# Sliding-window attention with sinks, followed by a GELU MLP: token pairs in the q/k loads, a new order of first loads, the first GEMM2 by row-block pairs, and DMA transposes

## The chip, the cores and the metric

The kernel runs on one core of one Trainium2 chip. The metric is the device time of one execution in microseconds. The kernel before took 263.49 us (median of 4 runs in the rounds shared with the changed kernel). Engine names are as in the profile: PE (TensorE matmuls), PEld (its weight loads), DVE (VectorE), ACT (ScalarE), POOL (GpSimd), SP (SyncE, whose queue issues nearly all DMAs; "SPq"). A **span** is the time from the first to the last instruction of a profiled run.

## The reference

Batch 4, 8 heads, 768 tokens, head size 64, in float32. Each query sees the last 128 keys and the first 4 ("sinks"). The result goes through an MLP with exact GELU.

```python
scores = scale * q @ k.T
keep   = is_sink | ((rel >= 0) & (rel < 128))
a      = softmax(where(keep, scores, -1e9))
x      = (a @ v)  -> (3072, 512)      # tokens x (head, dim)
out    = gelu(x @ w_in) @ w_out       # 512 -> 2048 -> 512
```

## The kernel before

Tokens are handled in 12 **groups** g of 256 tokens. Two groups make a **chunk** c of 512 tokens, so there are six chunks, 0 to 5. For each chunk, GEMM1 (64 matmuls, GELU on ACT) is followed by GEMM2 (64 matmuls), and the attention of the next chunk is interleaved in slots after every four matmuls of GEMM2. While GEMM1 of chunk c runs, q, k and v of chunk c+1 are cast to bf16, and q and k are transposed on PE:

```python
def qk_transpose(g, pp, eng=nc.vector):          # twice per group: 2 x 8 PE transposes
    ...
    nc.tensor.transpose(pt[:, a, w, e, :], src[:, e, 2*p:2*p+2, :]..., ident)
    ...
    copy(eng, qkt, pt)                           # PSUM -> SBUF, on DVE

def x_transpose(g, p):                           # per group and pair of heads: 2 PE transposes
    for e in range(2):
        nc.tensor.transpose(tp[:, e*P:(e+1)*P], x4[:, 2*e:2*e+2, :]..., ident)
    nc.vector.tensor_copy(out=XT[c][:, p, o:o+Q2], in_=tp)
```

Loads go through ten staging tiles of 512 KB, in the order of one list `stream`. `pump()` issues as many as have a free staging tile. A tile becomes free when its cast has been written into the program:

```python
def pump(limit=len(stream)):
    while head[0] < min(limit, len(stream)):
        n = head[0]
        if n >= NST and not freed[n - NST]: return
        ...                                      # q, k, v: two DMAs each, runs of 256 bytes
```

Instructions stay in program order on each engine, DMA issues on SP too.

The softmax here doesn't subtract the row's maximum and nothing guards it: scores larger than these inputs give would overflow.

## Time and profile before

| | kernel before |
|---|---|
| span of the profiled run | 261.3 us |
| GEMM1 of chunk 1 starts | 74.89 us |
| four periods (start of GEMM1 of chunks 1 to 5) | 39.4, 38.5, 37.8, 39.4 us |
| from GEMM1 of chunk 5 to the end | 31.2 us |
| PE busy | 88% |

The starts are read from the chain of waits, the profile's list of the work that led to the last instruction. A wait counts only if the engine that waits is on that chain at that time. Before 75 us that is mostly DMA, after it PE. The prediction below shows the lines.

### The profile page before, as it was taken

Reading aid. Unit: us, or ns where it says so; the run is one execution under the profiler, and the core shown is the slowest. Engines: PE = TensorE matmul, PEld = TensorE weight load, DVE = VectorE, ACT = ScalarE, POOL = GpSimd, SP = SyncE. Lnnn points to the kernel's source line nnn. Section 1 sums busy time; section 2 is a strip of 40 time slices with the busy share of each in tenths; the row PEclk is TensorE's granted clock in tenths of the full one; section 3 lists DMA queues with packets and bytes.
Section 4 is the critical chain, followed back from the end, with each engine's and each line's share of the span. In section 5 each row is a group of like instructions: output and inputs, shape, how many; then the busy total and the mean of one; then the engine's idle time right before and its main releaser. Section 6 shows DMA issues by size and latency. Waiting matters only on the chain.

```text
span 261.3 us, 4320 instructions
## 1 busy us (share of the span) xinstructions
PE 230.7 (88%) x1734; PEld 118.2 (45%) x1764; DVE 122.1 (47%) x277; ACT 115.4 (44%) x120; POOL 32.4 (12%) x82
## 2 busy tenths in 40 slices
PE   0467699869999989999999999999999989999994
PEld 0235445325445535444535444545445445544441
DVE  0284844247844256844346734357643267610111
ACT  0556336555315585314575325585135666136300
POOL 7177500690000000002000000200000000000000
PEclk9998589999999999999999999999999999999999
DMA  8999999999999991129920146001210010110022
GB/s 155 218 273 348 257 229 271 387 240 229 200 221 283 228 168 43 43 96 225 203 48 34 43 129 112 3 2 41 80 40 3 0 40 4 75 48 0 0 83 80
DMA packets 84756, 33.84 MB, mean 129 GB/s; under 512 B 75520, under 2 KB 79616, under 8 KB 84736
## 3 DMA queue, kind: packets, MB, share of 16 engines
q1 hardware_dynamic: 82656, 33.04, 54.8%
q10 hardware_dynamic: 2080, 0.52, 1.1%
q8 instruction: 14, 0.23, 0.4%
q14 instruction: 6, 0.05, 0.1%
HBM read 27.26 MB, written 6.29 MB: 128 GB/s over the span
## 4 chain that ended last, share of the span: by engine, by line
PE 58%; DMA 13%; DVE 8%; SPq 7%; ACT 7%; issue 5%; POOL 1%; another core or an unknown queue 0%; ACTq 0%; POOLq 0%; DVEq 0%
PE big L399 26%; PE po L418 21%; SPq L170 7%; ACT et L304 5%; DMA st<-in_moe_w_out_dram 5%; DMA st<-in_moe_w_in_dram 4%; DMA st<-in_v_dram 4%; PE qkps L244 3%; DVE osb L427 3%; PE big L295 2%; PE bank L383 2%; DVE x L368 1%; DVE et L315 1%; PE bank L356 1%; ACT gt L407 1%
## 5 line engine op out<-in xcount | busy, mean ns | idle before, releaser
L418 PE MATMUL po<-WOUT,gt 128*128 128x512 bf16 x365 | 91.5, 380 | 5.3 <-POOL WOUT L193 3.3
L399 PE MATMUL big<-xt,WIN 128*128 128x512 bf16 x373 | 88.0, 383 | 0.7 <-issue 0.2
L407 ACT ACTIVATE gt<-big 128x1024 bf16<-128x1024 f32 x48 | 49.1, 1023 | 88.4 <-PE big L399 87.2
L399 PEld LDWEIGHTS <-WIN 128*128 128x128 bf16 x384 | 37.0, 99 | 41.6 <-issue 2.4
L304 ACT ACTIVATE et<-big 128x1024 bf16<-128x1024 f32 (+1 forms) x48 | 44.5, 954 | 19.8 <-PE big L295 11.5
L418 PEld LDWEIGHTS <-gt 128*128 128x128 bf16 x384 | 33.1, 98 | 41.2 <-issue 10.9
L308 DVE TENSOR_TENSOR et<-et,mask 128x1024 bf16<-128x1024 bf16 x32 | 24.2, 758 | 28.7 <-ACT et L304 28.6
L427 DVE COPY osb<-po 128x512 f32<-128x512 f32 x24 | 16.5, 688 | 39.7 <-PE po L418 39.6
L193 DVE COPY qkt<-qkps 128x1024 bf16<-128x1024 bf16 x22 | 15.2, 691 | 35.3 <-PE qkps L244 35.3
L256 POOL COPY sk<-qkt 64x4 bf16<-64x4 bf16 x32 | 6.9, 215 | 129.0 <-DVE qkt L193 127.9
L244 PE MATMUL qkps<-ident,q 128*128 128x128 bf16 x96 | 13.2, 234 | 8.1 <-DVE q L193 7.9
L295 PE MATMUL big<-qkt 64*128 64x128 bf16 (+1 forms) x256 | 18.6, 249 | 2.0 <-ACT et L304 2.0
L368 DVE TENSOR_TENSOR x<-bank,rz 128x256 bf16<-128x256 f32 x44 | 18.7, 424 | 1.5
L356 PE MATMUL bank<-vo,et 128*128 128x65 bf16 x176 | 18.7, 198 | 0.2 <-POOL sk L256 0.2
L383 PE MATMUL bank<-ident,x 128*128 128x128 bf16 x88 | 12.9, 230 | 6.0 <-DVE x L368 5.9
L348 PE MATMUL bank<-vo,et 128*128 128x65 bf16 x148 | 17.2, 197 | 0.1
L383 PEld LDWEIGHTS <-x 128*128 128x128 bf16 x96 | 6.6, 101 | 22.5 <-DVE x L368 20.6
L356 PEld LDWEIGHTS <-et 128*128 128x128 bf16 x192 | 15.8, 103 | 2.0 <-issue 0.9
L348 PEld LDWEIGHTS <-et 128*128 128x128 bf16 x160 | 15.0, 103 | 0.9 <-DVE et L308 0.3
L244 PE MATMUL qkps<-ident,k 128*128 128x128 bf16 x96 | 13.2, 233 | 1.9 <-ACT k L191 1.9
L244 PEld LDWEIGHTS <-q 128*128 128x128 bf16 x96 | 8.9, 105 | 13.0 <-DVE q L193 7.9
L389 DVE COPY xt<-bank 128x256 bf16<-128x256 bf16 x44 | 12.5, 285 | 3.8 <-PE bank L383 3.8
(52 smaller groups left out, 146.5 us busy)
## 6 DMA issues: line engine op xcount, KB each, us to landing
st<-in_q_dram SPq DMA_DIRECT2D x24, 256.0 KB, 5.1
st<-in_v_dram SPq DMA_DIRECT2D x24, 256.0 KB, 4.9
out_dram<-osb SPq DMA_DIRECT2D x24, 256.0 KB, 2.0
st<-in_k_dram SPq DMA_DIRECT2D x22, 256.0 KB, 4.8
st<-in_moe_w_in_dram SPq DMA_DIRECT2D x8, 512.0 KB, 7.9
st<-in_moe_w_out_dram SPq DMA_DIRECT2D x8, 512.0 KB, 9.3
st<-in_k_dram ACTq DMA_DIRECT2D x2, 256.0 KB, 5.6
```

Source lines behind the costliest of these rows:

```text
L244: nc.tensor.transpose(pt[:, a, w, e, :], src[:, e, 2 * p : 2 * p + 2, :].rearrange("s h d -> s (h d)"), ident,)
L295: nc.tensor.matmul(ps[:, hl, c : c + n * P], lhsT=kb[r : r + D, :], rhs=qt(g, p)[r : r + D, e : e + n, :].rearrange("p e n -> p (e n)"), s ...
L304: nc.scalar.activation(out=et[:, :, c0:], in_=ps[:, :, c0:], func=AF.Exp, scale=att_scale)
L308: nc.vector.tensor_tensor(out=et.rearrange("p h (e n) -> p (h e) n", e=2), in0=et.rearrange("p h (e n) -> p (h e) n", e=2), in1=mask.unsqu ...
L348: nc.tensor.matmul(pov[:, e, hl, :], lhsT=et[:, hl, 2 * e * P : (2 * e + 1) * P], rhs=low[:, h, :], start=(i == 0), stop=False, skip_group ...
L356: nc.tensor.matmul(pov[:, e, hl, :], lhsT=et[:, hl, (2 * e + 1) * P : (2 * e + 2) * P], rhs=VO[g][:, e, h, :], start=(low is None), stop=True,
L368: nc.vector.tensor_tensor(out=x4, in0=pv4[:, :, 0:D], in1=rz.unsqueeze(2).to_broadcast((P, 4, D)), op=ALU.mult,)
L383: nc.tensor.transpose(tp[:, e * P : (e + 1) * P], x4[:, 2 * e : 2 * e + 2, :].rearrange("p h d -> p (h d)"), ident,)
L399: nc.tensor.matmul(ph[:, a, :], lhsT=WIN[:, t, ts(f, P)], rhs=XT[c][:, t, :], start=(t == 0), stop=(t == NKT - 1),)
L407: nc.scalar.activation(out=gt, in_=ph, func=AF.Gelu)
L418: nc.tensor.matmul(po, lhsT=GT[c, f // 2][:, f % 2, ts(m, P)], rhs=WOUT[:, f, :], start=(f == 0), stop=(f == NFT - 1),)
L427: nc.vector.tensor_copy(out=osb, in_=po)
```

## The change

The intent is to take transposes and copies off PE and DVE, to make loads cheaper, and to start sooner. The core of the diff, with cuts marked by "...":

```diff
-    for g in range(4):
-        stream += [("q", g), ("k", g), ("v", g)]
-    stream[6:6] = [("wi", j) for j in range(8)]
+    stream = [("q", 0), ("k", 0), ("q", 1), ("k", 1), ("v", 0), ("v", 1)]
+    stream += [("wi", j) for j in range(8)]
+    stream += [(kind, g) for g in (2, 3) for kind in "qkv"]
     stream += [("wo", j) for j in range(8)]
...
+                if kind == "v":                  # four DMAs of 64 partitions, every other row
+                    for e in range(2):
+                        for r in range(2):
+                            eng.dma_start(out=dst[HP*r : HP*(r+1), e, :, :],
+                                in_=src[:, e*P:(e+1)*P, :].rearrange("h (s r) d -> r s h d", r=2)[r])
+                else:                            # q, k: one DMA, two tokens per partition, 512 bytes
+                    eng.dma_start(out=st.rearrange("p (h c) -> p h c", h=H),
+                        in_=src.rearrange("h (p r) d -> p h (r d)", r=2))
...
+    def qk_dma(g):                               # groups 4 to 11: four per group
+        ...
+                nc.sync.dma_start(out=qkt[:, w, e]..., in_=cast["qk"[w], g][e*HP:(e+1)*HP]..., transpose=True)
...
+        elif p == NPAIR - 1:                     # in av(): x of groups 2 to 11, one per group
+            nc.sync.dma_start(out=xt_tile(g // 2)[:, o:o+2]..., in_=XG[g]..., transpose=True)
...
-            nc.sync.dma_start(out=out[r0 : r0 + P, :], in_=osb)
+            for r in range(2):                   # rows are even/odd tokens: two stores of 64 partitions
+                nc.sync.dma_start(out=out[r0 : r0 + P, :].rearrange("(s r) c -> r s c", r=2)[r],
+                    in_=osb[HP * r : HP * (r + 1), :])
...
+            if c == 0:   # after GEMM1 of chunk 0 has been emitted
+            mms = [(2 * a + m, f) for a in range(2) for f in range(NFT) for m in range(2)]
+        else:
+            mms = [(m, f) for m in range(4) for f in range(NFT)]
```

Constants are filled by DVE instead of POOL, and the exponential's table is loaded at the start. A function for warm-up matmuls is defined but never called.

## The prediction

> **What bounds the kernel now.** I read the page first: the busy row, then the 40 slices.
>
> ```profile
> PE   0467699869999989999999999999999989999994
> PEclk9998589999999999999999999999999999999999
> DMA  8999999999999991129920146001210010110022
> ```
>
> One slice is 261.3 / 40 = 6.5 us. After the first eight or so slices TensorE (PE) is nearly always busy; before that it is broken up. DMA is full for the first 15 slices (about 95 us), then mostly idle. So there are two regimes, and the 88% of PE on the page is an average over both. I cut the span at the starts of GEMM1 of each chunk, which the chain of waits gives (74.89, 114.33, 152.85, 190.67, 230.11 us), and asked for the busy time by stretch (columns: span, then PE, PEld, DVE, ACT, POOL busy, clock, DMA share, GB/s):
>
> ```profile
> 57.00:74.90 17.90, 16.62 (x152) 8.70 (x155) 11.72 (x33) 6.15 (x7) 1.30 (x5) 1.00 1.09 212
> 74.90:90.60 15.70, 15.60 (x96) 8.10 (x97) 7.07 (x11) 7.18 (x8) 0.00 (x0) 1.00 1.13 249
> 90.60:114.30 23.70, 22.11 (x213) 11.45 (x216) 13.37 (x35) 12.15 (x13) 0.00 (x0) 1.00 0.43 89
> 230.10:243.90 13.80, 13.75 (x65) 6.24 (x64) 0.69 (x1) 7.16 (x7) 0.00 (x0) 1.00 0.05 19
> ```
>
> A chunk's GEMM1 stretch (second row) is 15.7 us; the last chunk's (fourth row), which has no q/k transposes beside it, is 13.8 us, 64 matmuls at 0.216. The GEMM2-plus-attention stretch (third row) is 23.7 us, of which PE is idle 1.6. From 74.9 us on, PE sets the time: four chunk periods of 39.4, 38.5, 37.8 and 39.4 (mean 38.8), and a last stretch of 31.2.
>
> The idle 1.6 us has an owner. The waits of PE's weight loads, whole kernel:
>
> ```profile
> PEld L383 <- DVE x L368: 20.6, 37, 1.4
> ```
>
> L383 is the transpose of the attention output x. It waits on VectorE (DVE), which must mask, normalise and evict for the same slot.
>
> For the start I read the DMA queue's own order of issues (start, length, what):
>
> ```profile
> 40.38 5.00 SPq L180 DMA_DIRECT2D st<-in_moe_w_out_dram  x8
> 45.95 7.01 SPq L170 DMA_DIRECT2D st<-in_q_dram  x2
> ...
> 74.50 2.40 SPq L170 DMA_DIRECT2D st<-in_q_dram  x2
> 77.00 3.16 SPq L429 DMA_DIRECT2D out_dram<-osb  x4
> ```
>
> The first output tile was evicted by 59.5 us, yet its store is issued at 77.0: SyncE issues in program order, and ten loads (q4 to q7) stand in front. Today nobody waits for that store. I keep this in mind, because the change puts something urgent in its place.
>
> Rates, from the DMA view of 0 to 60 us in 40 slices of 1.5 us:
>
> ```profile
> GB/s 0 106 274 218 217 218 218 218 218 218 224 313 350 349 349 347 350 354 344 255 154 200 263 224 221 220 216 216 237 355 382 391 386 384 391 375 273 131 168 207
> ```
>
> The 218 plateaus are the q/k/v loads (256-byte runs), 350 is w_in (1 KB), 386 is w_out (2 KB). Per run and engine (16 x bytes / rate) this is 18.8, 46.8 and 84.9 ns, which is a straight line: 9.5 ns + 0.0367 ns per byte.
>
> **What the Trainium skill says.** (1) "DMA: Bandwidth & Descriptors", Specifications, gives 512 B as the minimum transfer for line rate. The trace agrees that 256 B is poor (218 against 386), but its line shows no step: it gives 28.3 ns, or 289 GB/s, at 512 B (estimate). (2) The same page, Queues, rings and completion order, says each DMA engine consumes its ring in order; the store at 77.0 us fits. (3) "Advanced Engine Details and Errata", X-Bar Transpose (TRN2), says transpose DMAs are as fast as regular ones, 350 to 400 GB/s, while the DMA page's table Latency and other measured facts has 261 GB/s for a non-contiguous case. This kernel has no such DMA, so no run here shows it; it is my weakest number. (4) "TensorE: Matmul & The Clock Gate", Part 1, says that after an idle window of about 3.4 us PE runs at half clock until about 3.4 us of work has passed. The trace agrees in kind: the granted clock is 0.59 between 30.5 and 36 us, after a stretch with gaps.
>
> **The change part by part.**
>
> *q/k transposes by DMA from chunk 2.* Groups 4 to 11 lose 8 x 16 = 128 PE transposes. The page's mean of 234 ns is latency; in the chain eight take 0.45 us, so a chunk saves 32 x 0.056 = 1.8 us of PE. This agrees with 15.7 - 13.8 = 1.9. All of it is on the path. Four chunks: 7.2 us. DVE also loses four 0.69 us copies per chunk, off the path.
>
> *x transposes by DMA from chunk 1.* 16 per chunk, a pair every 0.12 us in the timeline: 0.96 us of PE, on the path. With them goes the wait for DVE in front of them, about 1.5 us per chunk (PE idle of 1.6, 1.5, 1.1, 1.7 in the four GEMM2 stretches), and eight 0.285 us DVE copies. I count 2.4 us per chunk.
>
> So the period becomes 38.8 - 1.8 - 2.4 = 34.6 us; four periods save 17.
>
> *What comes back at each chunk start.* GEMM1 needs the whole x^T. The last AV is now in slot 11 of 16, followed by 20 matmuls x 0.216 = 4.3 us. Beside that run DVE's reciprocal and multiply (0.17 + 0.42, with hand-overs about 0.9), then SyncE's issue, and 256 KB through the transposer: 0.7 to 1.0 us by (3), plus about 2.0 us to landing, the page's median for a 256 KB store. That is 3.6 to 3.9 plus issue, against 4.3. I take 1 us lost per boundary, four boundaries: +4. The eight q/k transposes (128 KB each) have the 13.8 us of GEMM1 to hide in.
>
> *Token pairs and the new order.* A q or k tile of 512 KB costs 1.81 us in place of 2.41 (estimate from the line), 0.6 saved. v keeps 256-byte runs. SyncE must issue everything up to q7 before the first x transpose of chunk 1: the eight w_out casts pull in those loads before GEMM2(0) is emitted. Work in front: 15 q/k tiles x 1.81 + 7 v x 2.41 + 8 x 1.50 + 8 x 1.36 = 67.0 us, starting at 2. The same sum for the old kernel is 75.9 + 2 = 77.9, and its q7 finished issuing at 76.9, so the model holds. The new q7 is therefore in at about 69 to 70.5 us, and then come the transpose of group 2, two output tiles, and the transpose of group 3: x^T for chunk 1 at about 74, where GEMM1(1) starts at 74.9 today. By its own work PE would be ready at 62 to 66 (faster start of attention, no wait for w_out). It idles some 8 us, finds a halved clock and loses about 1.5. The better first loads thus buy almost nothing: 74 + 1.5 against 74.9.
>
> *GEMM2(0..4) by row-block pairs.* It lets the w_out blocks of chunk 0 be used as they land (waits of 3.3 us before w_out matmuls on the page), but that gain lies in the stretch which the queue now bounds. In later chunks it halves the pace at which GELU outputs are needed. Two evictions now fall together, covered by a slot of attention. I count 0.
>
> *Early Exp table load, memsets moved.* The 1.28 us table load at 7.9 us leaves the start; also absorbed. The warm-up function is defined and never called: 0.
>
> Sum: 74 + 1.5 + 4 x 34.6 + 4 + 31.2 = 249.1 us of span. The measured time is 263.88 - 261.3 = 2.6 above the span, so **251.7**.
>
> **Rivals.**
>
> A. The start is PE-bound after all: the x transposes are not held up behind loads, and GEMM1(1) begins at 62 to 66. For it: PE work alone ends there, and one fast queue would do it. Against: the store at 77.0. It would make about 240 to 243.
>
> B. DMA transposes are slow. At 3 us per 128 KB the eight q/k transposes take 24 us per chunk, SyncE's six loads (12 us) queue behind them, and the x transposes behind those: periods of 38 to 40 us, DMA taking PE's place as bound. For it: I have no measured duration. Against: both figures in (3). It makes 258 to 268.
>
> C. Transposes land in time but the masks and exponentials bind the GEMM2 stretch: exp 1.02 and DVE 0.69 + 0.17 + 0.42 = 1.28 us per slot, against 0.86 + 0.33 + 0.38 = 1.57 of PE. The margin is there, so at most 1 us per chunk: about 256.
>
> **Range and chances.** The period is certain to about 1 us (4 in all), the boundary wait 0 to 3 us each, the first x^T 70 to 78. Together 241 to 261. Below 258.6 is faster by 2%: only B, or C with a late start, prevents it. Faster 0.80, within 2% 0.16, slower 0.04.
>
> **What would show it.** GEMM1(1) starts at 72 to 76 us after several idle us of PE, released by a transpose DMA, with q7's load issued just before that; then periods of 34 to 36.5 us with GEMM1 stretches near 14 and hardly any PE wait on DVE's x; at each later chunk start a wait of about 1 us for the x transpose. The rate of q/k loads is near 289 GB/s. I am wrong if GEMM1(1) starts before 68 (A), if boundary waits exceed 3 us or attention waits for q/k transposes (B), or if exp or mask waits recur in the GEMM2 stretch (C).

## The result, and the profile after

The changed kernel took **255.38 us** (median of 4 runs, 254.93 to 256.1) against 263.49. The ratio is 0.9689, with a 95% interval of 0.9648 to 0.9729. It is the mean time of the one kernel's fast runs over that of the other's in the same rounds, so not quite the ratio of the medians. Executions over 1.5% slower than the fastest of the same kernel are left out of the means. The prediction was 251.7 with a range of 241 to 261. The direction and the range held, and the centre was 3.7 us too fast. (The profiled run was the slowest of the four: 256.1 us, span 254.1. The other spans were 252.9 to 253.5.)

The 40 slices of the changed kernel (6.35 us each):

```profile
PE   0686997878804999999999999999999999999992
PEclk9996899999965799999999999999999999999998
DMA  6999999999999579945669995593465213510133
```

Note the hole in PE in slices 12 and 13, the fallen clock in it and just after it, and the solid nines from there on. Here is the queue of SP around the hole (start, length, what):

```profile
70.08 0.98 SPq L195 DMA_DIRECT2D st<-in_q_dram  x1
71.16 2.72 SPq L428 DMA_TRANSPOSE xt<-xg  x1
73.98 2.47 SPq L484 DMA_DIRECT2D out_dram<-osb  x4
76.54 1.31 SPq L428 DMA_TRANSPOSE xt<-xg  x1
77.95 2.46 SPq L484 DMA_DIRECT2D out_dram<-osb  x4
```

L428 is the x transpose. Its first input was ready at 59.5 us, its second at 65.6 (the ends of the last multiply of groups 2 and 3 on DVE). They are issued at 71.16, right behind the load of q of group 7, and at 76.54, behind four stores. PE's waits say what this costs (who waited for whom, us in total, times, longest):

```profile
PE big L455 <- DMA xt<-xg: 10.5, 1, 10.5
```

There is one such wait in the whole kernel, 10.5 us long. The stretches from there on (span, then PE, PEld, DVE, ACT, POOL busy, clock, DMA share, GB/s):

```profile
79.68:96.35 16.67, 16.67 (x65) 6.95 (x65) 0.00 (x0) 7.16 (x7) 0.00 (x0) 0.83 0.72 143
...
117.98:132.20 14.22, 14.22 (x67) 6.26 (x65) 4.99 (x8) 7.16 (x7) 0.38 (x2) 1.00 0.59 97
132.20:152.34 20.14, 19.86 (x174) 9.89 (x172) 11.02 (x27) 11.04 (x12) 0.00 (x0) 1.00 1.19 220
```

The first row is GEMM1 of chunk 1: 16.67 us at a mean granted clock of 0.83, where 64 matmuls at full clock take 13.8. The other two are GEMM1 and GEMM2 of chunk 2: 14.2 and 20.1 us, with 0.28 us of idle PE in the latter. The chain of waits gives the starts of GEMM1 of chunks 2 to 5:

```profile
117.98 6.91 PE big L455 x32
...
152.34 6.91 PE big L455 x32
...
186.23 13.83 PE big L455 x64
...
221.51 13.81 PE big L455 x64
```

| | before | predicted | after |
|---|---|---|---|
| GEMM1 of chunk 1 starts | 74.89 | 74 | 79.68 |
| lost to the clock in it | 0 | 1.5 | 2.87 (16.67 - 13.8) |
| four periods, without that loss | 155.2 | 138.4 | 138.96 (35.43, 34.36, 33.89, 35.28) |
| waits at later chunk starts | - | 4 | 0 |
| last stretch | 31.2 | 31.2 | 32.6 |
| span | 261.3 | 249.1 | 254.1 |

The periods gave 16 us. The start took back 4.8, the clock 2.9 and the end 1.4.

### The profile page after: what moved, and what is told of

Read it like the earlier page. It is cut to its first block, busy times and chain, and to the rows that moved or that the text cites. A ratio compares the mean times of both kernels' runs of the same rounds, so it can differ in the third digit from the quotient of the medians.

```text
span 254.1 us, 3961 instructions
## 1 busy us (share of the span) xinstructions
PE 220.4 (87%) x1556; PEld 109.0 (43%) x1556; DVE 103.2 (41%) x237; ACT 114.8 (45%) x120; POOL 28.9 (11%) x47
## 4 chain that ended last, share of the span: by engine, by line
PE 61%; SPq 17%; DMA 11%; DVE 5%; issue 2%; ACT 2%; POOL 1%; DVEq 0%; ACTq 0%
PE po L472 30%; PE big L455 22%; SPq L188 7%; DMA st<-in_moe_w_in_dram 6%; SPq L296 4%; PE big L340 4%; SPq L195 3%; DMA st<-in_v_dram 2%; DMA st<-in_moe_w_out_dram 2%; SPq L484 2%; PE bank L404 2%; DVE osb L481 2%; ACT et L349 2%; PE bank L396 1%; PE bank L384 1%
## 5 line engine op out<-in xcount | busy, mean ns | idle before, releaser
L455 PE MATMUL big<-xt,WIN 128*128 128x512 bf16 x384 | 87.2, 388 | 10.5 <-DMA xt<-xg 10.5
L472 PE MATMUL po<-WOUT,gt 128*128 128x512 bf16 x384 | 93.4, 380 | 3.3 <-POOL WOUT L218 2.4
L472 PEld LDWEIGHTS <-gt 128*128 128x128 bf16 x384 | 33.3, 97 | 42.2 <-issue 10.2
L481 DVE COPY osb<-po 128x512 f32<-128x512 f32 x24 | 16.3, 688 | 40.3 <-PE po L472 34.7
L418 DVE TENSOR_TENSOR xg<-bank,rz 128x256 bf16<-128x256 f32 x44 | 18.7, 424 | 1.5
L360 DVE TENSOR_TENSOR et<-et,mask 128x768 bf16<-128x768 bf16 x16 | 9.0, 566 | 15.2 <-ACT et L349 14.6
L263 POOL COPY sk<-qkt 64x16 bf16<-64x16 bf16 x8 | 2.1, 269 | 111.1 <-DMA qkt<-k 110.8
L384 PE MATMUL bank<-vsk,ets 128*128 128x130 bf16 x60 | 12.3, 225 | 2.4 <-DVE vsk L251 1.3
L340 PEld LDWEIGHTS <-qkt 64*128 64x128 bf16 x256 | 7.7, 96 | 10.8 <-issue 7.5
L218 POOL CAST WOUT<-st 128x1024 bf16<-128x1024 f32 x8 | 9.4, 1186 | 15.0 <-DMA st<-in_moe_w_out_dram 14.8
L218 POOL CAST WIN<-st 128x1024 bf16<-128x1024 f32 x8 | 9.4, 1172 | 3.8 <-DMA st<-in_moe_w_in_dram 3.8
L415 DVE RECIPROCAL rz<-bank 128x4 f32<-128x4 f32 x44 | 7.8, 177 | 4.5 <-PE bank L404 3.9
L218 DVE CAST q<-st 128x1024 bf16<-128x1024 f32 x11 | 7.5, 686 | 4.9 <-DMA st<-in_q_dram 4.9
```

Of the source, the lines that this page charges most:

```text
L218: eng.tensor_copy(out=out, in_=in_)
L340: nc.tensor.matmul(ps[:, hl, c : c + n * P], lhsT=kt(gk, p, ek, rows), rhs=qt(g, p, e, n, rows), start=True, stop=True,)
L418: nc.vector.tensor_tensor(out=XG[g][:, :, 2 * p : 2 * p + 2, :], in0=pov[:, :, :, 0:D], in1=rz.rearrange("p (e h) -> p e h", e=2).unsqueez ...
L455: nc.tensor.matmul(ph[:, a, :], lhsT=WIN[:, t, ts(f, P)], rhs=XT[c][:, :, t, :], start=(t == 0), stop=(t == NKT - 1),)
L472: nc.tensor.matmul(po, lhsT=GT[c, f // 2][:, f % 2, ts(m, P)], rhs=WOUT[:, f, :], start=(f == 0), stop=(f == NFT - 1),)
L481: nc.vector.tensor_copy(out=osb, in_=po)
```

## The experiments

Each is an edit of the changed kernel, and each ratio is to the kernel before. "Start" below is the start of GEMM1 of chunk 1, 79.68 us in the changed kernel.

**e1_cap: fewer loads in front of the x transposes.** Is it the order in SP's queue?

```diff
                 take("wo", j, G_)
-                pump()
+                pump(32)          # also in the two side slots of chunk 0
...                                # after GEMM2 of chunk 0:
+        if c == 0:
+            pump(34)
...                                # in later chunks, side slot 1: pump() -> pump(34 + 6 * c)
```

> Edit: in chunk 0 the loads are capped so that only q4, k4, v4, q5 stand in front of the x transposes of chunk 1 on SyncE; k5 and v5 follow after the stores of chunk 0, later groups six per chunk. Theory Q (in-order queue): GEMM1 of chunk 1 starts at 69 to 71 us in place of 79.7, finds a warm clock and takes 13.9 us in place of 16.7; the span falls by 10 to 13 us to 241 to 244, ratio to the kernel before 0.92 to 0.93. Rival T (the transposes themselves are slow when the first ones run): the start stays at 77 us or later and the gain is under 3 us. Rival D (DMA bandwidth is the bound, the loads are only moved): the wait comes back as a wait for k5/v5 or for the q/k transposes in chunk 1, and the gain is under 5 us.

Measured: 246.56 us (three runs within 0.3 us, a fourth at 249.71), ratio 0.9378 (0.9317 to 0.9439), correct, span 244.5. SP's queue and the chain:

```profile
56.92 1.18 SPq L195 DMA_DIRECT2D st<-in_q_dram  x1
59.82 1.35 SPq L428 DMA_TRANSPOSE xt<-xg  x1
61.46 2.46 SPq L484 DMA_DIRECT2D out_dram<-osb  x4
65.87 1.23 SPq L428 DMA_TRANSPOSE xt<-xg  x1
```
```profile
69.48 13.83 PE big L455 x64
...
107.53 7.08 PE big L455 x32
```

The transposes are issued as soon as x is there, the start is 10.2 us earlier, and GEMM1 takes 13.83 us. The bytes loaded are the same. So the wait was one of order, as theory Q says. No run separates the order in which SP issues from the order in the DMA queue behind it. The gain stays just under the forecast 10 us (9.6 of span), because PE waits 2.8 us for x at the start of chunk 2: six loads, which now run later (SP issues them from 87 to 100 us), stand in front of that one.

**e2_x_pe: the x transposes of chunk 1 on PE.** The urgent work leaves the queue altogether.

```diff
-        if g < 2:
+        if g < 4:                 # and x_transpose(g, p) one slot after av(g, p)
             PO[g, p] = po
```

> Edit: the x transposes of chunk 1 alone (groups 2 and 3) are done by PE again; the order of loads is that of the changed kernel. Theory Q: nothing on PE's path hangs on SyncE's queue at the start, so GEMM1 of chunk 1 starts at 70 to 72 us; it pays 1 to 2.5 us for 16 PE transposes and their waits for DVE; the q/k transposes of group 4 are still issued only at about 80 us and may hold GEMM2 of chunk 1 by up to 3 us. Net gain 6 to 11 us, span 243 to 248. Rival T: about the same, since no transpose stands at the start. Rival D: under 5 us, because the loads still take the queue until 71 us and something else waits for them.

Measured: ratio 0.9404 (0.9352 to 0.9456), correct. The two fast runs took 248.8 and 247.2 us. The profiled run was slow (251.0), so its span is not compared. In it GEMM1 of chunk 1 starts at 70.55 us, as theory Q says (first line, from the chain), and this wait of PE appears for chunk 2 (second line):

```profile
70.55 13.83 PE big L456 x64
...
PE big L456 <- DMA xt<-xg: 5.1, 1, 5.1
```

With the loads untouched, the backlog meets the next x transposes instead. That would explain why it gains less than e1_cap, but I have the wait only from that slower run.

**e3_fill: dummy matmuls in the hole.** Is the slow GEMM1 of chunk 1 the clock?

```diff
+        if c == 0:
+            warm_up(86)           # after GEMM2 of chunk 0
```

> Edit: 86 dummy matmuls of 256 columns (0.107 us each, 9.2 us) fill PE's idle time before GEMM1 of chunk 1; nothing else changes. Theory K (the clock fell during the 10.5 us of idle PE): GEMM1 of chunk 1 takes 13.8 to 14.0 us in place of 16.7 and the span falls by 2.5 to 3 us, ratio 0.957 to 0.962. Rival: if the 2.9 us come from something else (contention of the q/k transposes with PE's reads, or DVE casts), the span stays within 0.5 us.

Measured: 254.85 us, ratio 0.9664 (0.9631 to 0.9698), correct, span 252.8. The timeline of PE:

```profile
71.51 9.55 PE L497 MATMUL po<-mask,ident 128*128 128x256 bf16 x86 [0.56 <-DVE osb L481]
80.89 13.98 PE L455 MATMUL big<-xt,WIN 128*128 128x512 bf16 x64
```

GEMM1 takes 13.98 us in place of 16.67: theory K holds, and the 2.7 us were the clock. The span fell by only 1.3, because GEMM1 now begins at 80.89, 1.2 us after the old start. Two things came later in this run: the second x transpose, issued at 76.56, took 3.9 us to land (80.5, against 79.6 in the changed kernel), and the fill, which began after a GEMM2 of chunk 0 that ended later, ran to 81.06. The forecast of 2.5 to 3 for the span was missed for that reason.

**e4_qk_pe: q and k on PE again, x on DMA.** What was the first part worth?

```diff
-    0: lambda: (casts(ga), qk_dma(ga)),
-    1: lambda: (casts(gb), qk_dma(gb), pump()),
+    0: lambda: casts(ga), 1: lambda: qk_transpose(ga, 0), 2: lambda: (qk_transpose(ga, 1), ...),
+    4: lambda: (casts(gb), pump()), 5: lambda: qk_transpose(gb, 0), 6: ...
```

> Edit: q and k are transposed by PE in all chunks, as in the kernel before; x still by DMA. Prediction's term: 32 transposes of 0.056 us per chunk = 1.8 us in each of four chunks, so the span rises by 7 to 8 us to 261 to 262, ratio 0.995 to 1.00. Rival: the eight q/k transposes per chunk load the queue and the DMA engines so much that taking them away gives part of it back; then the rise is under 5 us.

Measured: 262.08 us, ratio 0.9937 (0.9911 to 0.9963), correct, span 259.6: 5.5 us more. The periods are 38.6, 36.0, 35.7 and 37.1. Against the changed kernel (38.3, 34.4, 33.9, 35.3) the last three rise by 1.7, 1.8 and 1.8, which is the predicted 1.8. The first rises by only 0.3: GEMM1 of chunk 1 with its transposes ends after 17.0 us at a mean clock of 0.92, so a smaller loss to the clock hides most of the cost there. That is why the span rose by 5.5 and not by the forecast 7 to 8. The starts of GEMM1 of chunks 3 to 5 in this run:

```profile
154.64 3.45 PE big L455 x16
...
190.32 3.45 PE big L455 x16
...
227.39 13.81 PE big L455 x64
```

**e5_v_plain: v as before (wrong result).** Why was q7 late?

```diff
-    for e in range(2):
-        for r in range(2):
-            eng.dma_start(out=dst[HP*r : HP*(r+1), e, :, :], in_=...[r])
+    for e in range(2):
+        eng.dma_start(out=dst[:, e, :, :], in_=src[:, e*P:(e+1)*P, :].rearrange("h s d -> s h d"))
```

> Wrong result on purpose: v is loaded as in the kernel before (two DMAs of 128 partitions, rows in plain order) instead of four DMAs of 64 partitions that pick every other row. Theory V: the new pattern of v is slower (about 197 GB/s in its plateau against 218 before), 0.25 us for each of the seven v tiles in front of the first x transpose, so GEMM1 of chunk 1 starts 1.5 to 2 us earlier, at about 78 us, and the span falls by as much, to about 252.3. Rival: the q/k runs of 512 bytes are to blame for the late q7; then the start moves by less than 0.5 us.

Measured: 252.73 us, ratio 0.9563 (0.9508 to 0.9618), wrong rows, span 250.7. The start is 76.26 us, 3.4 earlier. Here is the DMA view of 0 to 60 us in slices of 1.5 us, first of the changed kernel, then of this one:

```profile
GB/s 0 74 308 302 291 289 259 194 196 201 289 348 348 350 348 350 350 348 314 293 251 163 127 273 286 228 199 221 330 389 392 382 388 389 369 310 290 203 205 204
```
```profile
GB/s 0 81 299 307 291 291 267 218 217 235 345 347 350 349 345 354 350 341 297 288 235 165 239 315 268 221 336 389 392 376 391 386 386 339 292 280 224 164 329 298
```

From the third slice come q and k (289 to 308 GB/s), then v (194 to 201, against 217 and 218), then w_in. So the pattern of v costs more than I had thought. A tile of 512 KB takes 2.66 us at 197 GB/s and 2.41 at 217.5, so the plateau alone explains 0.25 us per tile, 1.75 for seven. SP's queue shows more: against this run the changed kernel issues its first w_in load 0.9 us later (12.42, 11.56; two v tiles in front), its first w_out load 2.5 later (38.45, 35.93; four) and q7 4.3 later (70.08, 65.81; seven). That is 0.4 to 0.6 us per v tile. Why it is more than 0.25 is not shown. The 512-byte runs are at the estimated rate, so the rival falls.

**e6_store: one store per output tile (wrong result).**

```diff
-            for r in range(2):
-                nc.sync.dma_start(out=...[r], in_=osb[HP*r : HP*(r+1), :])
+            nc.sync.dma_start(out=out[r0 : r0 + P, :], in_=osb)
```

> Wrong result on purpose: each output tile is stored by one DMA of 128 partitions in plain row order, as in the kernel before, instead of two DMAs of 64 partitions. Theory S: the last tile's second store is issued 0.55 us later and lands 0.4 us slower, so the stretch from the last matmul to the end goes back from 5.0 to about 3.6 us; the first x transpose of group 3 also comes about 1.2 us sooner, because one issue per tile instead of two stands in front of it. Span down by 2 to 3 us to about 251.5. Rival: stores cost nothing because the ring is the bound; then under 1 us.

Measured: 253.96 us, ratio 0.9616 (0.9567 to 0.9665), wrong rows, span 251.6. The starts of the last eviction (DVE timeline) in the kernel before, in the changed one and in this one:

```profile
257.78 0.69 DVE L427 COPY osb<-po 128x512 f32<-128x512 f32 x1 [2.76 <-PE po L418]
```
```profile
249.18 0.69 DVE L481 COPY osb<-po 128x512 f32<-128x512 f32 x1 [2.76 <-PE po L472]
```
```profile
247.56 0.69 DVE L481 COPY osb<-po 128x512 f32<-128x512 f32 x1 [2.76 <-PE po L472]
```

To the ends of the spans (261.3, 254.1, 251.6) that is 3.5, 4.9 and 4.0 us, so the split store explains 0.9 of the 1.4 us at the end. The span fell by the forecast 2 to 3 us, but less than half of that (0.9) for a forecast reason. At the start theory S fails: the second x transpose is issued 0.8 us sooner but takes 3.8 us to land instead of 3.1, and GEMM1 of chunk 1 starts at 79.59. The stores' issue time was not the bound there. Of the 2.5 us of span, 1.35 come from a GEMM1 of chunk 1 that lost only 1.5 us to the clock. That is luck: the loss differs between kernels that all have a hole there (1.5 here, 1.9 in e7_morder, 1.8 in e10_x_pe_later, 2.9 in the changed kernel, 3.1 in e5_v_plain).

**e7_morder and e8_cap_morder: GEMM2 of chunk 0 row block by row block**, in the changed kernel and in e1_cap.

```diff
-            mms = [(2 * a + m, f) for a in range(2) for f in range(NFT) for m in range(2)]
-        else:
-            mms = [(m, f) for m in range(4) for f in range(NFT)]
+        mms = [(m, f) for m in range(4) for f in range(NFT)]
```

> Edit: GEMM2 of chunk 0 runs row block after row block as in the kernel before, not by pairs. Prediction: worth 0 here, since the start of GEMM1 of chunk 1 is set by SyncE's queue; span 254 +/- 0.5. Rival: the pairs shorten the stretch that matters, then the span rises by 1.5 us or more.

> Edit: the capped loads of e1_cap, with GEMM2 of chunk 0 row block after row block. With the queue out of the way GEMM2 of chunk 0 is on the path: row block 0 needs all eight w_out blocks in its first 16 matmuls, the last of which lands at about 51 us. Theory: GEMM1 of chunk 1 starts 1.5 to 3 us later than in e1_cap (69.5), at 71 to 72.5 us, span 246 to 247.5. Rival: the pairs are worth nothing here either, because the two evictions that fall together cost what they save; then within 0.5 us of e1_cap.

Measured: e7_morder 255.01 us, ratio 0.9653 (0.9606 to 0.9699), span 253.5, start 80.14. The start is 0.5 us later, and GEMM1 of chunk 1 lost 0.9 us less to the clock. The pairs are worth next to nothing while the queue sets the start, as predicted. e8_cap_morder: 249.46 us, ratio 0.9442 (0.9389 to 0.9495), span 247.2, start 70.91 against 69.48 in e1_cap. So with the queue out of the way they are worth 1.4 us at the start, a little under the forecast of 1.5 to 3; the rest of the 2.7 us of span is mostly a GEMM1 of chunk 2 whose first half took 8.59 us in place of 7.08. Both are correct.

**e10_x_pe_later: x on PE in chunks 2 to 5.** What was the second part worth?

```diff
-        if g < 2:
+        if g < 2 or g >= 4:       # and x_transpose(g, p) one slot after av(g, p)
             PO[g, p] = po
```

> Edit: x is transposed by PE in chunks 2 to 5 and by DMA in chunk 1 only; q and k stay on DMA. Prediction's term: 2.4 us per chunk (0.96 of PE, about 1.5 of waits for DVE) in four periods, so the span rises by 9 to 10 us to 263 to 264. Rival: the waits for DVE do not come back, because DVE no longer has the q/k copies; then only the 0.96 us of PE return, 4 us, span 258.

Measured: 265.00 us, ratio 1.0028 (0.9979 to 1.0078), correct, span 262.9: 8.8 us more. The periods are 39.5, 36.7, 36.3 and 37.7; the last three are 2.4 above those of the changed kernel each, which is the predicted term. The first includes a smaller loss to the clock (1.8). The starts of GEMM1 of chunks 3 to 5, and the wait, which is back:

```profile
156.38 6.91 PE big L455 x32
...
192.69 13.83 PE big L455 x64
...
230.35 13.81 PE big L455 x64
...
PEld L437 <- DVE xg L418: 18.0, 30, 1.7
```

In the changed kernel the same row has 3.3 us (4 times), from chunk 0. So the rival (DVE is now free enough) falls.

**e9_best and e11_best2: a combination.** e1_cap, and further: two of each chunk's six loads go behind the stores of its GEMM2, and v of group 3 is loaded after six of the w_out blocks. e9_best also issues half of the last stores from ACT. e11_best2 drops that and forms the sink values later.

```diff
+    stream += [("q", 2), ("k", 2), ("v", 2), ("q", 3), ("k", 3)]
+    stream += [("wo", j) for j in range(6)] + [("v", 3)] + [("wo", j) for j in range(6, 8)]
...                                                                  # v of group 3 is also cast later
...
-                    1: lambda: (casts(gb), qk_dma(gb), pump()),
+                    1: lambda: (casts(gb), qk_dma(gb), pump(32 + 6 * c)),
-                    3: lambda: [sink_values(b) for b in sv],
+                    7: lambda: [sink_values(b) for b in sv],        # e11_best2 only
...                                                                  # after GEMM2 of every chunk:
+        pump(34 + 6 * c)
```

> A combination: the cap of e1_cap; two of each chunk's six loads moved behind its GEMM2's stores (so that no x transpose waits behind them: 2.8 us in chunk 2 of e1_cap); v of group 3 loaded and cast after most of w_out (w_out is then 2 us earlier); the second half of the last chunk's stores issued from ScalarE. Expected by the parts: 244.5 - 2.8 - 2 - 0.5 = 239 us of span, ratio 0.915 to 0.925. If the moved loads make the q/k transposes late, the gain stays under 2 us against e1_cap.

> As e9_best, but the sink values are formed after the last instead of the fourth pair of GEMM1 in chunks 2 and on, and all stores are on SyncE again. In e9_best PE waited 3.2 us (at 144 to 147 us) for the cast of the late v of group 9 there. Theory: that wait was the price of the loads moved back, so the span falls by 3 us to about 239, ratio 0.91 to 0.92. Rival: the late k and v are also waited for by the q/k transposes and the attention, then the wait moves to the GEMM2 stretch and the gain is under 1 us. The stores of the last chunk: no change, the stretch from the last eviction's start to the end stays 4.9 us.

Measured: e9_best's three fast runs took 243.72 to 245.33 us (the fourth, 248.63, was slow), ratio 0.9275 (0.9226 to 0.9324), span 242.0, correct. That is 3 us short of the 239 expected. The start is 67.21 us (2.3 earlier than in e1_cap, as expected), and the wait for x in chunk 2 is gone. But this wait of PE was new:

```profile
PE bank L244 <- DVE vo L218: 3.2, 1, 3.2
```

It is the matmul of the sink values, placed in the middle of GEMM1, behind the cast of a v that now lands late. The stores from ACT changed nothing: 242.0 - 237.08 = 4.9 us from the last eviction to the end. e11_best2 removed the wait, as its theory says: **241.14 us** (median of 6 fast runs, 239.72 to 242.24), ratio 0.9135 (0.9103 to 0.9167), span 238.6, correct.

## Why the prediction was right or wrong

**The period was right, by its own steps.** 34.6 us was predicted and the mean of four is 34.7 without the clock loss. Both terms hold where nothing covers them: 1.8 us per chunk for q/k (e4_qk_pe: 1.7, 1.8, 1.8) and 2.4 for x with its waits (e10_x_pe_later: 2.4 three times). They are shown, not only argued.

**The mechanism at the start was right.** The prediction read, in a store that nobody waited for, that SP issues in program order, and said that the x transposes would stand behind those loads and that "the better first loads thus buy almost nothing". e1_cap shows it: with the same work in another order the start moves by 10.2 us. (The prediction sets that store beside what the skill says of rings, its point 2. What it shows is SP's order of issue; no trace here looks into the rings.)

**The size at the start was off: the term "q7 is therefore in at about 69 to 70.5".** x^T came at 79.7, outside the prediction's own 70 to 78. q7 was issued at 70.08 and landed 5.7 us later, at about 75.8. From there to x^T it took 3.9 us, as the prediction's next term has it (about 4). Two things were wrong in the term. First, it priced v at the old 2.41 us, though the diff splits v into four DMAs with another pattern: with the old pattern (e5_v_plain) the start is 3.4 us earlier. Second, it checked its sum for the kernel before (77.9) against the end of q7's issue (76.9), not against its landing. That kernel's q7 loads took a median of 5.0 us to land, so the last was in near 80.7 (75.7, half-way through the two issues, + 5.0), and the sum falls some 2.8 short. That the two together make up the miss is argued from these numbers; no run adds them up.

**When PE would be ready was off too:** 62 to 66 predicted, 69.2 measured (79.68 less the wait of 10.49). In e1_cap, where GEMM1 of chunk 1 waits for no transpose, it starts at 69.48. So with the queue out of the way PE's own work sets the start, some 3 us later than the prediction's latest figure. Why is not shown. Since x^T was later still, this did not change the time; the hole was 10.5 us in place of "some 8".

**The clock term was half the size:** 1.5 predicted, 2.87 in the profiled run, 1.5 to 3.1 over the runs. The cause is shown by e3_fill. The prediction took about 3.4 us of work at half clock from the skill, its point 4. In the changed kernel the granted clock is 0.50 from 79.68 to 84.68 us and 0.60 in the next microsecond, so half clock held for about 5.8 us.

**The wait of 1 us at each later boundary did not come:** 0, not 4. A lone x transpose needs 1.23 us of issue and lands 3.1 us after its issue began. The term took DVE 0.9, then 2.7 to 3.0 (of which 0.7 to 1.0 was an estimate from the skill's rates, its point 3) plus the issue beyond it, while in the trace the issue lies inside the 3.1. In chunk 2 the last one was issued at 114.37 and in at 117.4, against a need at 118.0. It fits by half a microsecond, by the changed kernel's trace alone.

**The end was not predicted:** +1.4 us. The split store was in the diff and I gave it nothing. e6_store shows 0.9 of it.

**A misreading:** the prediction speaks of "GEMM2(0..4) by row-block pairs", but the diff has pairs in chunk 0 only. It was valued at 0 and is worth 0 (e7_morder), so no number changes. That it would help only with the queue gone is confirmed by e8_cap_morder.

The errors sum as 5.7 (start) + 1.4 (clock) - 4 (boundaries) + 0.6 (periods) + 1.4 (end) = 5.1 us, against 254.1 - 249.1 = 5.0. In measured time the miss is 3.7: the profiled run was 0.7 above the median, and the prediction added 2.6 for time outside the span where 2.0 was measured. (The 2.6 set the median of the kernel before against another run's span; the run profiled there took 263.17, 1.9 above its span.) The range held because errors of both signs met, which is luck. Nor is 241 to 261 the sum of its parts: the three ranges added at their ends give about 240 to 268. **The rivals:** A (240 to 243, a PE-bound start) was not what happened. The right order of issues does give a start that PE sets (e1_cap), but at 69.5 us and not at 62 to 66, and 244.5 us of span. B (slow transposes) fell: the q/k transposes took 2.6 to 4.3 us each to land, eight of them occupied SP's queue for 10.5 us per chunk, and no attention waited for one. C fell too: in the GEMM2 stretches of chunks 1 to 4 PE was idle for 0.3 us or less each.

## What to carry to other kernels

When work moves from an engine to a DMA queue, write down what stands in front of it in that queue at the moment it becomes urgent. An in-order queue turns cheap early prefetches into a wait, and capping them can be worth as much as the change itself (here 9 us beside 8). Calibrate a sum of transfers against the landing of the last one, not against its issue, and price every transfer whose access pattern the diff touches again. When loads are moved back to clear the way, look for the small consumer that is placed early, like the sink values here.

## What the Trainium skill lacked or had wrong

- "Advanced Engine Details and Errata", X-Bar Transpose (TRN2), says transpose DMAs are as fast as regular DMAs, 350 to 400 GB/s. Here, from SBUF to SBUF, the DMA view shows 200 to 220 GB/s while an x transpose moves, the rate of 256-byte packets. The 261 GB/s in the table of "DMA: Bandwidth & Descriptors" is nearer.
- The skill has a time for a transpose by DMA of one 128x128 block only ("VectorE: DVE Perf Modes", The three transpose paths). No page gives the time from issue to landing of larger ones. Here SP was occupied for about 1.25 us per transpose, equally for 128 KB (64 partitions) and 256 KB (128 partitions), and they landed 2.7 and 3.1 us (medians) after the start of the issue.
- "DMA: Bandwidth & Descriptors", Specifications, gives 512 B as the minimum for line rate. Here 512 B was not enough, and the rate went on rising: 218, 289 to 308, 350 and 386 GB/s for runs of 256 B, 512 B, 1 KB and 2 KB.
- The same page, Rules for kernel authors, says of two transfers to disjoint partition halves "Don't bother", because they serialize. That is borne out, and the cost can be stated: splitting the last store made the end 0.9 us longer, and v in four quarters ran at 194 to 201 GB/s in place of 218.
- "TensorE: Matmul & The Clock Gate", Part 1, warns that the ramp penalty varies. It does: after a hole of 6.4 to 10.5 us GEMM1 lost 1.5 to 3.1 us. e10_x_pe_later, whose edit lies wholly behind this point, lost 1.8 after a hole of 8.9, the changed kernel 2.9 after 10.5. That is 0.6 to 1.2% of this span, where the page has under 1%. By the granted clock, half speed held for about 2.7 us of work in e6_store and 5.9 in e5_v_plain, where the page has about 3.4.
